# A gated linear attention and an MLP on one core: another order of work, constants as immediates, a divided last tile

## The chip, the core and the metric

The kernel runs on one core of one Trainium2 chip. A core has five engines with a queue of instructions each, worked through in order: TensorE (matrix products, the profile's PE, its weight loads PEld), VectorE (DVE), ScalarE (ACT), GpSimd (POOL) and SyncE (SP), which here only issues transfers. TensorE writes to eight PSUM banks; VectorE and ScalarE read them. The metric is the device time of one execution in microseconds, lower is better, given as the median of several runs.

## What is computed

```python
# attention, per batch (4) and head (8), 768 steps, head dim 48
mag   = sqrt(a_re**2 + a_im**2)
scale = minimum(mag, 0.999) / (mag + 1e-6)
a     = (a_re + i*a_im) * scale              # per step and channel
S     = a[t][:, None] * S + outer(k[t], v[t])   # complex state 48 x 48
y[t]  = q[t] @ real(S)
# MLP over x = the heads' y side by side (384 columns)
xn  = (x - mean(x)) / sqrt(var(x) + 1e-6) * g_ln
out = x + maximum(xn @ w_ch1, 0) @ w_ch2     # 384 -> 1536 -> 384
```

The kernel doesn't step through time. It takes the logarithm of the magnitude and the angle of every gate, sums both along time with products by triangular matrices of ones, and turns the recurrence into masked products of scaled q and k within chunks of 128 steps, with a 48 x 48 state carried from chunk to chunk.

## The kernel before, in words

The 3072 rows (4 batches of 768) are 24 chunks of 128, taken as 12 pairs, three to a batch. An operation's name tells what it does and for which pair P or chunk n; pair 0 does its gate work in two halves of four heads (are.0.0 and are.0.1), the others in one piece (are.1.0). In the order in which they depend on each other:

- **Loads (SP)**: are, aim, q, k, vf. **Gates**: ln, iv, r, r2, u, l, lc (ScalarE's logarithms and exponentials, products on VectorE or GpSimd) give the log magnitude; th is the angle (ScalarE).
- **Sums along time (TensorE)**: dec (log magnitude, products with u_e) and ph (angle; pick adds the carry car of the pair before). From their PSUM banks ScalarE makes e and en (exponentials), sin and cos (qt adds a quarter turn for the pairs 0 to 3; later pairs take the absolute value, abs). Logarithm and exponential are in one table of ScalarE, sine and arctangent in another; tab.log and tab.trig switch it.
- **Attention**: ke = k*en, qe = q*e, ks and qs (times sin and cos), v (cast). kT and qT are eight transposes each on TensorE, ksT and qsT copy them out of PSUM (some by a transposing transfer on SP instead). am are the scores, atm masks them, gm and G (with dps, decc, gs) make the state, y is the output of a chunk, x its copy.
- **MLP**: bn, rstd (normalisation), xtr and xT (transpose of x). mm1.P.g.part are the first layer's 36 products a pair (128 x 256) in three groups g, relu.P.g empties a group, mm2.n.part are a chunk's 12 products of 384 columns, ot (on VectorE; or oa on ScalarE and ot on GpSimd) scales and adds x, st stores.
- **Weights**: wl.0 loads the first layer's weights (w1b) and wl.1 the second's (w2b), both issued by GpSimd; gln is the layer norm's gain. wgc makes the matrix gc from it, wp.0 to wp.2 multiply w1b by it, and nine wc (VectorE) rewrite w1b with the gain and mean folded in. mm1 of a group waits for its three wc.
- **warm.i** are fillers: products of ones into a bank that nobody reads.

The order isn't computed by the kernel: PLAN is a table of tokens `name:engine+bank@behind`. The engines' letters are P, A, V, G and S; the number is the first PSUM bank; `@` puts a GpSimd instruction behind one of another engine. Each engine executes its tokens in the table's order, with the waits that the data, the rings of buffers (RINGS) and the banks need. Rows of the profile carry the lines of the helpers: 291 is every two-operand product of VectorE or GpSimd, 286 and 288 the copies of ScalarE and VectorE, 445 ln, 447 iv, 459 u, 463 l, 466 lc, 474 dec, 478 e and en, 482 th, 489 and 493 ph, 503 and 506 car, 511 sin, 518 qt, 522 and 534 cos, 588 kT and qT, 611 am, 672 and 675 y, 693 xtr, 726 mm1, 737 and 739 relu, 747 mm2, 761 and 759 ot, 776 the fillers, 781 the table switches, 381 wp, 385 wc, 372 gc, 361 and 363 the weights' loads, 709 and 710 rstd.

## Time and profile before

| | |
|---|---|
| median of 3 runs (lowest, highest) | 187.94 us (187.75, 189.71) |
| the profiled execution, in all | 189.19 us |
| its span, first to last instruction | 187.5 us |
| TensorE busy | 178.7 us, 95% (fillers 17.3 us of it, 128 instructions) |
| VectorE, ScalarE, GpSimd busy | 155.4, 158.3, 93.4 us |
| ScalarE's table switches | 17, 21.8 us |
| first weights' load, issue to landing | 12.0 us (second: 10.9) |
| moved by DMA | 36.08 MB, 192 GB/s in the mean |

A row of instructions in the profile reads: line, engine, operation, output<-inputs, shapes, count | busy time, mean ns of one | idle time of the engine ahead of them and what ended it. A window's row has the busy time of each engine with the number of its instructions in brackets, in the order TensorE, its weight loads, VectorE, ScalarE, GpSimd, then TensorE's granted clock, the DMA engines' share and GB/s. The chain of waits is followed back from the last instruction; its rows are start, length and what. Matmuls are pipelined: a busy time of TensorE says that one is under way, not that the array is full.

### The profile page before, as it was taken

What the parts mean: (1) busy time and instruction counts of PE and PEld (TensorE: products, weight loads), DVE (VectorE), ACT (ScalarE), POOL (GpSimd) and SP (SyncE); (2) the same over time, 40 slices, a digit from 0 to 9 for tenths busy, and PEclk for the clock granted to TensorE, in tenths of its full rate; (3) what the DMA queues carried; (4) which work ended last, traced back from release to release, by engine and by line L of the source; (5) the groups of instructions that cost most, each with busy time, mean ns of one, the idle gap of its engine ahead of it and who ended that gap; (6) DMA issues with size and microseconds to landing.
All of it is one profiled execution on the core that took longest, in us unless ns stands there. A gap on an engine that the chain in (4) does not pass through costs nothing.

```text
span 187.5 us, 5175 instructions
## 1 busy us (share of the span) xinstructions
PE 178.7 (95%) x2066; PEld 139.7 (75%) x2066; DVE 155.4 (83%) x292; ACT 158.3 (84%) x219; POOL 93.4 (50%) x117
## 2 busy tenths in 40 slices
PE   5889997999999999999999999999999999999992
PEld 3777676578866787887887887877877878787771
DVE  0379999799998999998899899999889878399431
ACT  3999999699999899999999999998999884527440
POOL 8411229756363297576572955175754174170110
PEclk9999999999999999999999999999999999999998
DMA  5999999799999998489999999996979989994223
GB/s 153 285 225 187 246 190 185 170 220 174 239 210 240 223 267 208 85 195 236 203 209 251 162 232 247 196 217 158 189 159 240 178 159 186 184 170 123 85 84 126
DMA packets 126183, 36.08 MB, mean 192 GB/s; under 512 B 121168, under 2 KB 125776, under 8 KB 126160
## 3 DMA queue, kind: packets, MB, share of 16 engines
q1 hardware_dynamic: 124208, 33.40, 84.6%
q0 software_dynamic: 1952, 2.36, 7.7%
q8 instruction: 16, 0.26, 0.6%
q14 instruction: 7, 0.06, 0.1%
HBM read 28.31 MB, written 4.72 MB: 176 GB/s over the span
## 4 chain that ended last, share of the span: by engine, by line
PE 80%; DMA 8%; ACT 7%; DVE 2%; issue 1%; DVEq 0%
PE banks L726 25%; PE banks L747 25%; DMA w1b<-in_moe_w_ch_dram 6%; PE banks L588 5%; PE banks L611 5%; PE banks L493 3%; PE banks L474 3%; PE banks L672 2%; PE banks L693 2%; PE banks L675 2%; PE banks L635 2%; DMA are<-in_a_re_dram 2%; PE banks L489 2%; ACT w L445 1%; ACT are L447 1%; ACT L781 1%
## 5 line engine op out<-in xcount | busy, mean ns | idle before, releaser
L747 PE MATMUL banks<-w2b,h 128*128 128x384 bf16 x288 | 52.5, 326 | 0.0
L726 PE MATMUL banks<-xT,w1b 128*128 128x256 bf16 x432 | 52.2, 272 | 0.0
L726 PEld LDWEIGHTS <-w1b 128*128 128x128 bf16 x432 | 41.2, 98 | 5.6
L747 PEld LDWEIGHTS <-h 128*128 128x128 bf16 x288 | 26.4, 97 | 14.9 <-ACT h L737 0.2
L737 ACT ACTIVATE h<-banks 128x1024 bf16<-128x1024 f32 x28 | 28.1, 1021 | 10.2 <-PE banks L726 9.9
L291 DVE TENSOR_TENSOR atm<-banks,mask 128x1024 bf16<-128x1024 f32 x24 | 29.2, 1218 | 4.6 <-PE banks L611 4.5
L291 POOL TENSOR_TENSOR ke<-k,en 128x384 bf16<-128x384 f32 x19 | 17.3, 915 | 17.1 <-DVE qs L291 6.9
L781 ACT ACT_TABLE_LOAD x17 | 21.8, 1283 | 1.1 <-PEq L797 0.8
L291 POOL TENSOR_TENSOR qe<-q,e 128x384 bf16<-128x384 f32 x17 | 15.4, 915 | 12.0 <-DVE qs L291 3.6
L776 PE MATMUL banks<-u_e 128*128 128x256 f16 x128 | 17.3, 290 | 2.3 <-POOL u_e L325 2.2
L776 PEld LDWEIGHTS <-u_e 128*128 128x128 f16 x128 | 12.6, 104 | 5.4 <-POOL u_e L325 1.9
L291 POOL TENSOR_TENSOR r<-aim,are 128x768 f16<-128x768 f32 x7 | 12.7, 1816 | 6.7 <-ACT are L447 5.0
L759 POOL TENSOR_TENSOR ot<-ot,x 128x384 f32<-128x384 f32 x8 | 7.3, 913 | 17.4 <-ACT ot L752 15.6
L611 PE MATMUL banks<-qsT,ksT 128*128 128x128 bf16 x192 | 14.3, 219 | 0.2 <-ACT h L737 0.2
L685 DVE BATCH_NORM_STATS2 stats<-x 128x6 f32<-128x384 bf16 x24 | 13.1, 546 | 0.0
L611 PEld LDWEIGHTS <-ksT 128*128 128x128 bf16 x192 | 12.0, 98 | 1.3 <-issue 0.5
L493 PE MATMUL banks<-th,u_th 128*128 128x384 f16 (+1 forms) x52 | 11.8, 313 | 0.9 <-ACT th L482 0.9
L761 DVE SCALAR_TENSOR_TENSOR ot<-banks,rstd,x 128x384 f32<-128x384 f32 x16 | 9.7, 610 | 3.4 <-PE banks L747 3.3
L291 POOL TENSOR_TENSOR ks<-ke,trig 128x768 bf16<-128x768 bf16 x6 | 9.8, 1640 | 5.3 <-DVE l L466 2.4
L463 DVE SCALAR_TENSOR_TENSOR l<-r,w 128x768 f16<-128x768 f16 (+1 forms) x13 | 11.5, 890 | 0.9 <-ACT r L459 0.9
L672 PE MATMUL banks<-v,atm 128*128 128x48 bf16 x192 | 12.2, 183 | 0.0
L445 ACT ACTIVATE w<-are 128x768 f32<-128x768 f32 (+1 forms) x13 | 10.1, 788 | 2.4 <-DMA are<-in_a_re_dram 2.3
(97 smaller groups left out, 376.5 us busy)
## 6 DMA issues: line engine op xcount, KB each, us to landing
k<-in_k_dram SPq DMA_DIRECT2D x24, 192.0 KB, 4.1
q<-in_q_dram SPq DMA_DIRECT2D x24, 192.0 KB, 4.2
vf<-in_v_dram SPq DMA_DIRECT2D x24, 192.0 KB, 4.2
out_dram<-ot SPq DMA_DIRECT2D x24, 192.0 KB, 3.3
are<-in_a_re_dram SPq DMA_DIRECT2D x11, 384.0 KB, 4.8
aim<-in_a_im_dram SPq DMA_DIRECT2D x11, 384.0 KB, 4.5
w1b<-in_moe_w_ch_dram POOLq DMA_DIRECT2D x1, 1152.0 KB, 12.0
w2b<-in_moe_w_ch_dram POOLq DMA_DIRECT2D x1, 1152.0 KB, 10.9
```

The costliest lines, as they stand in the source:

```text
L291: {"DVE": nc.vector, "POOL": nc.gpsimd}[eng(name)].tensor_tensor(**kw)
L445: add(f"ln.{X}", lambda S_=S_: act(out=S_("w"), in_=S_("are"), func=AF.Ln), needs=[f"are.{X}"], uses=[("are", P), ("w", P)])
L463: nc.vector.scalar_tensor_tensor(out=S_("l"), in0=S_("r2"), scalar=0.5, in1=S_("w"), op0=ALU.mult, op1=ALU.add)
L493: nc.tensor.matmul(heads(ps[:, c]), lhsT=u_th[:, c, j], rhs=step(T("th", P), j), start=False, stop=(j == R - 1), skip_group_check=True)
L611: nc.tensor.matmul(ps[:, h], lhsT=T("ksT", n)[:, h], rhs=T("qsT", n)[:, h], start=True, stop=True)
L672: nc.tensor.matmul(ps[:, h], lhsT=T("atm", n)[:, h], rhs=T("v", P)[:, c, h], start=True, stop=nfirst)
L685: nc.vector.bn_stats(out=T("stats", n), in_=T("x", n))
L726: nc.tensor.matmul(ps[:, jj], lhsT=w1b[:, dc, ts(gi * JG + jj, C)], rhs=T("xT", P)[:, dc].rearrange("p c t -> p (c t)"), start=(dc == 0), ...
L737: act(out=dst, in_=src, func=AF.Relu)
L747: nc.tensor.matmul(bank(f"o.{n}")[:, 0:DM], lhsT=T("h", P)[:, j, ts(c, C)], rhs=w2b[:, j], start=(j == 0), stop=(j == NJ - 1))
L776: g.add(f"warm.{i}", lambda i=i: nc.tensor.matmul(bank(f"warm.{i}")[:, 0:256], lhsT=u_e[:, 0, 0], rhs=u_e[:, 1].rearrange("p j t -> p (j t ...
L781: g.add(f"tab.{nm}.{i}", lambda tab=tab: nc.scalar.preload_act_table_set(tab))
```

## The change

1. PLAN is another table. 128 fillers become 29: 14 of 256 columns as before and 15 of 512 (warm.w0 to warm.w14), the first of them behind lc.1.0. Many operations change their engine: of VectorE's ReLUs there are 12, not 8; of GpSimd's qs 6, not 2; r2 goes to ScalarE six times, not twice; table switches are 15, not 17. wl.0 stands behind ke.0.0.0 (before: l.2.0), and th.1.0 ahead of the second table switch (before: behind the third).
2. The activations' constants 1, pi/2 and 1e-6 are given as numbers, no longer as 128 x 1 tiles (one_b, quarter, eps_b).
3. wgc can be done by GpSimd in one instruction, and the new table does so.
4. The last chunk's second layer is done in two column pieces, 0 to 255 (mm2.23, ot.23, st.23) and 256 to 383 (mm2.24, ot.24, st.24), in two banks with two stores.

```diff
 PLAN = """
-are.1.0:S ue:G are.0.1:S are.0.0:S pad.ks.1:G zdec:G pad.ks.0:G k.0.1:S qrow:G car0.1:G pick:G aim.0.1:S tab.log.0:A
-ln.1.0:A mask:G aim.0.0:S one:G iv.1.0:A car0.0:G aim.1.0:S cmean:G pad.ks.2:G ln.0.1:A ident:G ln.0.0:A are.2.0:S
-iv.0.1:A iv.0.0:A gln:S r.0.1:V uth:V aim.2.0:S r.0.0:V r2.0.1:V r2.0.0:V tab.trig.1:A th.0.1:A th.0.0:A k.1.0:S
...
-warm.41:P0 warm.42:P0 ph.0.1:P2 r.1.0:V ph.0.0:P0 r2.1.0:V k.0.0:S tab.log.2:A u.0.1:A pad.qs.0:G@r2.1.0 q.0.0:S
-u.0.0:A l.0.1:V u.1.0:A vf.0.0:S l.0.0:V lc.0.1:V lc.0.0:V ln.2.0:A warm.43:P1 warm.44:P1 warm.45:P1 warm.46:P1
...
-warm.57:P1 warm.58:P1 warm.59:P1 warm.60:P1 warm.61:P1 warm.62:P1 warm.63:P1 dec.0.1:P5 l.1.0:V q.0.1:S dec.0.0:P4
-en.0.1:A5 lc.1.0:V e.0.1:A5 q.1.0:S car.0.1:V2 iv.2.0:A warm.64:P1 warm.65:P1 warm.66:P1 warm.67:P1 warm.68:P1
-dec.1.0:P6 pad.qs.1:G@lc.1.0 car.0.0:V0 q.1.1:S e.0.0:A4 r.2.0:V e.1.0:A6 vf.0.1:S en.0.0:A4 r2.2.0:V warm.69:P1
-warm.70:P1 warm.71:P1 warm.72:P1 warm.73:P1 warm.74:P1 warm.75:P1 warm.76:P1 warm.77:P1 warm.78:P1 dps.1:P5 dps.0:P1
-en.1.0:A6 ke.0.0.0:V are.3.0:S decc.1:V5 u.2.0:A qe.0.1.0:V k.1.1:S ke.0.1.0:V qe.1.0.0:V aim.3.0:S qe.0.0.0:V l.2.0:V
-tab.trig.3:A th.1.0:A q.2.1:S wl.0:G@l.2.0 lc.2.0:V sin.0.1:A2 warm.79:P3 warm.80:P3 warm.81:P3 warm.82:P3 warm.83:P3
...
-warm.103:P3 warm.104:P3 warm.105:P3 warm.106:P3 warm.107:P3 warm.108:P3 warm.109:P3 ph.1.0:P6 wgc:V sin.0.0:A0
-th.2.0:A decc.0:V1 k.2.0:S qs.0.1.1:V dec.2.0:P4 ke.1.0.0:V car.1.0:A6 qt.0.1:P2 ks.0.0.1:V sin.1.0:A6 qt.0.0:P0
-qe.1.0.1:V qs.0.0.1:V cos.0.0:A0 warm.110:P1 warm.111:P1 qt.1.0:P6 v.0:V cos.0.1:A2 ks.0.1.1:V cos.1.0:A6 ks.0.0.0:V
-qs.0.0.0:V qs.0.1.0:V ks.0.1.0:V warm.112:P0 warm.113:P0 warm.114:P0 warm.115:P0 warm.116:P0 warm.117:P0 warm.118:P0
-warm.119:P0 warm.120:P0 warm.121:P0 qT.0:P6 qs.1.0.1:V kT.1:P1 qs.1.0.0:V qT.1:P7 qsT.0:V6 tab.log.4:A ln.3.0:A
-ke.1.0.1:G@qs.1.0.0 kT.0:P0 qsT.1:V7 qT.2:P6 en.2.0:A4 ks.1.0.1:G@qs.1.0.0 qT.3:P2 ksT.1:V1 e.2.0:A4 gm.0:P7 ksT.0:V0
-iv.3.0:A warm.122:P3 warm.123:P3 warm.124:P3 am.1:P4 qsT.3:V2 ks.1.0.0:G am.0:P0 G.0:A7 atm.1:V4 ph.2.0:P2 vf.1.1:S
-atm.0:V0 gm.1:P7 y.1:P4 tab.trig.5:A sin.2.0:A2 k.2.1:S r.3.0:G G.1:V7 warm.125:P5 warm.126:P5 warm.127:P5 wp.2:P5
-qsT.2:A6 x.1:V4 y.0:P0 vf.1.0:S qt.2.0:P2 wc.2.2:V5 x.0:A0 wp.1:P7 cos.2.0:A2 wc.2.0:V5 aim.4.0:S qe.2.0.1:G xtr.1:P0
-kT.2:P1 wc.1.0:V7 xT.1:A0 xtr.0:P6 r2.3.0:G are.4.0:S th.3.0:A wp.0:P2 wc.2.1:V5 kT.3:P3 ksT.2:A1 q.2.0:S wc.1.2:V7
-ph.3.0:P4 wc.1.1:V7 ke.2.0.0:G xT.0:A6 vf.2.0:S ksT.3:A3 am.2:P0 wc.0.2:V2 v.1:G mm1.0.1.1:P6 atm.2:V0 sin.3.0:A4
...
-mm1.11.0.0:P0 ot.19:G ot.20:V2 st.18:S mm1.11.0.1:P0 bn.23:V st.20:S mm1.11.1.0:P4 st.19:S relu.11.0:A0 mm1.11.1.1:P4
-mm1.11.2.1:P6 relu.11.1:V4 mm1.11.2.0:P6 mm2.22.0:P0 relu.11.2:A6 mm2.22.1:P0 rstd.11:A mm2.22.2:P0 oa.21:A3
-mm2.23.0:P2 ot.22:V0 ot.21:G mm2.23.1:P2 st.22:S mm2.23.2:P2 st.21:S ot.23:V2 st.23:S
+ue:G are.1.0:S are.0.0:S are.0.1:S pick:G aim.1.0:S pad.qs.1:G qrow:G car0.1:G pad.ks.0:G aim.0.0:S tab.log.0:A
+ln.1.0:A pad.ks.2:G aim.0.1:S mask:G iv.1.0:A ident:G k.1.0:S ln.0.0:A cmean:G ln.0.1:A zdec:G car0.0:G pad.qs.0:G
+iv.0.1:A vf.0.0:S iv.0.0:A k.0.1:S r.1.0:V are.2.0:S r.0.0:V tab.trig.1:A th.1.0:A r.0.1:V gln:S uth:V th.0.0:A
+r2.0.1:V r2.0.0:V th.0.1:A ph.0.0:P1 aim.2.0:S r2.1.0:G@r2.0.0 ph.0.1:P0 q.0.1:S car.0.1:V0 car.0.0:V1 tab.log.2:A
+u.0.0:A u.0.1:A l.0.0:V q.0.0:S u.1.0:A lc.0.0:V l.0.1:V dec.0.0:P2 vf.0.1:S lc.0.1:V en.0.0:A2 l.1.0:V k.0.0:S
+ln.2.0:A lc.1.0:V iv.2.0:A q.1.1:S warm.w0:P3 warm.0:P3 warm.1:P3 dec.1.0:P4 pad.ks.1:G@lc.1.0 e.0.0:A2 r.2.0:V
+ph.1.0:P6 q.1.0:S en.1.0:A4 e.1.0:A4 dec.0.1:P2 r2.2.0:V k.1.1:S qe.0.0.0:V e.0.1:A2 car.1.0:V6 are.3.0:S en.0.1:A2
+warm.w1:P3 warm.2:P3 warm.3:P3 dps.0:P4 v.0:V u.2.0:A qe.0.1.0:V aim.3.0:S decc.0:V4 ke.0.1.0:V q.2.0:S ke.0.0.0:V
+wl.0:G@ke.0.0.0 l.2.0:V tab.trig.3:A sin.0.1:A0 q.2.1:S sin.0.0:A1 warm.w2:P3 warm.w3:P3 warm.4:P3@u.2.0 warm.w4:P3
+warm.w5:P3 warm.w6:P3 warm.w7:P3 warm.w8:P3 warm.5:P3 warm.6:P3 warm.7:P3 qt.0.1:P0 sin.1.0:A6 dps.1:P4 lc.2.0:V
+qt.0.0:P1 ks.0.0.1:V dec.2.0:P2 qs.0.1.1:V cos.0.0:A1 qe.1.0.0:V cos.0.1:A0 qt.1.0:P6 qs.0.0.1:V th.2.0:A qs.0.0.0:V
+qs.0.1.0:V ks.0.1.1:V cos.1.0:A6 warm.w9:P0 warm.8:P0 warm.9:P0 qT.1:P0 ks.0.0.0:V ks.0.1.0:V qT.0:P1 qsT.1:V0
+decc.1:A4 ke.1.0.0:G@ks.0.1.0 kT.1:P5 qsT.0:V1 kT.0:P6 gm.0:P0 qe.1.0.1:V tab.log.4:A e.2.0:A2 qs.1.0.0:V ksT.1:V5
+G.0:A0 ke.1.0.1:G@qs.1.0.0 en.2.0:A2 ksT.0:V6 warm.w10:P1 warm.w11:P1 warm.w12:P1 warm.w13:P1 warm.w14:P1 warm.10:P1
+warm.11:P1 warm.12:P1 gm.1:P0 am.1:P4 ks.1.0.0:V ln.3.0:A ph.2.0:P2 ks.1.0.1:V iv.3.0:A atm.1:V4 qs.1.0.1:G@ks.1.0.1
+kT.3:P6 kT.2:P7 G.1:V0 y.1:P4 ksT.2:V7 am.0:P0 wgc:G tab.trig.5:A sin.2.0:A2 qT.2:P5 k.2.0:S atm.0:V0 x.1:A4
+warm.13:P7 qt.2.0:P2 xtr.1:P4 qsT.2:V5 cos.2.0:A2 wp.1:P7 vf.1.1:S r.3.0:G xT.1:V4 y.0:P0 ksT.3:A6 wc.1.2:V7 am.2:P2
+vf.1.0:S qT.3:P1 wc.1.1:V7 x.0:A0 wp.0:P4 pad.qs.2:G k.2.1:S wc.1.0:V7 th.3.0:A xtr.0:P0 wp.2:P5 r2.3.0:G atm.2:V2
+qsT.3:A1 are.4.0:S ph.3.0:P6 xT.0:A0 wc.2.1:V5 aim.4.0:S am.3:P2 qe.2.0.1:G car.3.0:A6 mm1.0.1.0:P0 wc.2.0:V5
+sin.3.0:A6 are.5.0:S mm1.0.1.1:P0 atm.3:V2 wl.1:G@mm1.0.1.0 v.1:A qt.3.0:P6 vf.2.0:S relu.0.1:A0 ke.2.0.0:G wc.2.2:V5
...
+mm1.11.1.1:P0 oa.20:A3 st.21:S mm1.11.0.0:P4 ot.20:G mm1.11.0.1:P4 ot.19:G st.20:S mm1.11.1.0:P0 relu.11.0:A4
+mm1.11.2.1:P2 st.19:S relu.11.1:V0 mm1.11.2.0:P2 mm2.22.0:P4 relu.11.2:A2 mm2.22.1:P4 rstd.11:A mm2.22.2:P4
+mm2.23.0:P5 ot.22:V4 mm2.23.1:P5 st.22:S mm2.23.2:P5 mm2.24.0:P0 ot.23:V5 mm2.24.1:P0 mm2.24.2:P0 st.23:S ot.24:V0
+st.24:S
@@ -235,6 +226,7 @@
     ND = DM // C
     HALF = C // R
     JG = 4
+    CUT = 256
     NG = NJ // JG
     INV2PI = 1.0 / (2.0 * PI)
 
@@ -302,10 +294,7 @@
     u_e = pool.tile([C, R, R, C], FP16, name="u_e")
     pick = pool.tile([C, C], FP16, name="pick")
     mask = pool.tile([C, C], BF16, name="mask")
-    one_b = pool.tile([C, 1], FP32, name="one_b")
-    quarter = pool.tile([C, 1], FP32, name="quarter")
     half_n = pool.tile([C, R], FP32, name="half_n")
-    eps_b = pool.tile([C, 1], FP32, name="eps_b")
     qrow = pool.tile([C, DM], FP16, name="qrow")
     cmean = pool.tile([C, C], FP32, name="cmean")
     gc = pool.tile([C, ND, C], BF16, name="gc")
@@ -314,10 +303,7 @@
     w2b = pool.tile([C, NJ, DM], BF16, name="w2b")
 
     def c_one():
-        nc.gpsimd.memset(one_b, 1.0)
-        nc.gpsimd.memset(quarter, PI / 2)
         nc.gpsimd.memset(half_n, -0.5)
-        nc.gpsimd.memset(eps_b, 1e-6)
 
     def c_ue():
         nc.gpsimd.memset(u_e, 1.0)
@@ -365,6 +351,10 @@
     g.add("gln", lambda: nc.sync.dma_start(out=gln, in_=moe_g_ln.rearrange("(dc p) -> p dc", p=C)))
 
     def wgc():
+        if eng("wgc") == "POOL":
+            nc.gpsimd.tensor_tensor(out=gc, in0=cmean.unsqueeze(1).to_broadcast([C, ND, C]),
+                                    in1=gln.unsqueeze(2).to_broadcast([C, ND, C]), op=ALU.mult)
+            return
         for dc in range(ND):
             if eng("wgc") == "ACT":
                 nc.scalar.mul(out=gc[:, dc], in_=cmean, mul=gln[:, ds(dc, 1)])
@@ -456,8 +446,8 @@
                 else:
                     tt(f"r2.{X}", out=S_("r2"), in0=S_("r"), in1=S_("r"), op=ALU.mult)
             add(f"r2.{X}", f_r2, needs=[f"r.{X}"], uses=[("r", P), ("r2", P)])
-            add(f"u.{X}", lambda S_=S_: act(out=S_("r2"), in_=S_("r2"), func=AF.Ln, bias=one_b),
-                needs=[f"r2.{X}", "one"], uses=[("r2", P)])
+            add(f"u.{X}", lambda S_=S_: act(out=S_("r2"), in_=S_("r2"), func=AF.Ln, bias=1.0),
+                needs=[f"r2.{X}"], uses=[("r2", P)])
 
             def f_l(S_=S_):
                 nc.vector.scalar_tensor_tensor(out=S_("l"), in0=S_("r2"), scalar=0.5, in1=S_("w"),
@@ -533,8 +523,8 @@
                 add(f"abs.{X}", f_abs, needs=[f"ph.{X}"], uses=[("sh", P)], ps=(f"ph.{X}", nb))
                 add(f"cos.{X}", lambda fs=fs: act(
                     out=T("trig", P)[:, 0, :, fs], in_=T("sh", P)[:, :, fs], func=AF.Sin,
-                    scale=-TWO_PI_SAFE / TURN, bias=quarter),
-                    needs=[f"abs.{X}", "one"], uses=[("sh", P), ("trig", P)])
+                    scale=-TWO_PI_SAFE / TURN, bias=PI / 2),
+                    needs=[f"abs.{X}"], uses=[("sh", P), ("trig", P)])
 
 
             for nm, src, dc_ in (("ke", "k", "en"), ("qe", "q", "e")):
@@ -706,7 +696,7 @@
         def f_rstd():
             t = T("rstd", P)
             if eng(f"rstd.{P}") == "ACT":
-                act(out=t, in_=T("mv", P)[:, :, 1], func=AF.Ln, bias=eps_b)
+                act(out=t, in_=T("mv", P)[:, :, 1], func=AF.Ln, bias=1e-6)
                 act(out=t, in_=t, func=AF.Exp, scale=-0.5)
                 return
             nc.gpsimd.tensor_scalar(out=t, in0=T("mv", P)[:, :, 1], scalar1=1e-6, scalar2=None,
@@ -741,41 +731,48 @@
                 needs=[f"mm1.{P}.{gi}.0", f"mm1.{P}.{gi}.1"], uses=[("h", P)], ps=(o, 2))
         for c in range(R):
             n = P * R + c
-            for part in range(NG):
-                def f_mm2(n, c, part):
-                    for j in range(part * JG, part * JG + JG):
-                        nc.tensor.matmul(bank(f"o.{n}")[:, 0:DM], lhsT=T("h", P)[:, j, ts(c, C)],
-                                         rhs=w2b[:, j], start=(j == 0), stop=(j == NJ - 1))
-                add(f"mm2.{n}.{part}", lambda n=n, c=c, part=part: f_mm2(n, c, part),
-                    needs=[f"relu.{P}.{part}", "wl.1"] + ([f"mm2.{n}.{part - 1}"] if part else []),
-                    uses=[("h", P)], ps=(f"o.{n}", 1))
-            add(f"oa.{n}", lambda n=n, c=c: nc.scalar.mul(
-                out=T("ot", n), in_=bank(f"o.{n}")[:, 0:DM], mul=T("rstd", P)[:, ds(c, 1)]),
-                needs=[f"mm2.{n}.{NG - 1}", f"rstd.{P}"], uses=[("rstd", P), ("ot", n)],
-                ps=(f"o.{n}", 1))
-
-            def f_ot(n, c):
-                if eng(f"ot.{n}") == "POOL":
-                    nc.gpsimd.tensor_tensor(out=T("ot", n), in0=T("ot", n), in1=T("x", n), op=ALU.add)
-                else:
-                    nc.vector.scalar_tensor_tensor(
-                        out=T("ot", n), in0=bank(f"o.{n}")[:, 0:DM], scalar=T("rstd", P)[:, ds(c, 1)],
-                        in1=T("x", n), op0=ALU.mult, op1=ALU.add)
-            add(f"ot.{n}", lambda n=n, c=c: f_ot(n, c),
-                needs=[f"oa.{n}", f"mm2.{n}.{NG - 1}", f"rstd.{P}", f"x.{n}"],
-                uses=[("rstd", P), ("x", n), ("ot", n)], ps=(f"o.{n}", 1))
-            add(f"st.{n}", lambda n=n, c=c: nc.sync.dma_start(
-                out=out[b].rearrange("(c p) e -> p c e", p=C)[:, pp * R + c], in_=T("ot", n)),
-                needs=[f"ot.{n}"], uses=[("ot", n)])
+            tail = P == NP - 1 and c == R - 1
+            for N, ws in (((n, slice(0, CUT)), (n + 1, slice(CUT, DM))) if tail else ((n, slice(0, DM)),)):
+                for part in range(NG):
+                    def f_mm2(n, N, ws, c, part):
+                        for j in range(part * JG, part * JG + JG):
+                            nc.tensor.matmul(bank(f"o.{N}")[:, ws], lhsT=T("h", P)[:, j, ts(c, C)],
+                                             rhs=w2b[:, j, ws], start=(j == 0), stop=(j == NJ - 1))
+                    add(f"mm2.{N}.{part}", lambda n=n, N=N, ws=ws, c=c, part=part: f_mm2(n, N, ws, c, part),
+                        needs=[f"relu.{P}.{part}", "wl.1"] + ([f"mm2.{N}.{part - 1}"] if part else []),
+                        uses=[("h", P)], ps=(f"o.{N}", 1))
+                add(f"oa.{N}", lambda n=n, N=N, ws=ws, c=c: nc.scalar.mul(
+                    out=T("ot", n)[:, ws], in_=bank(f"o.{N}")[:, ws], mul=T("rstd", P)[:, ds(c, 1)]),
+                    needs=[f"mm2.{N}.{NG - 1}", f"rstd.{P}"], uses=[("rstd", P), ("ot", n)],
+                    ps=(f"o.{N}", 1))
+
+                def f_ot(n, N, ws, c):
+                    o, xs = T("ot", n)[:, ws], T("x", n)[:, ws]
+                    if eng(f"ot.{N}") == "POOL":
+                        nc.gpsimd.tensor_tensor(out=o, in0=o, in1=xs, op=ALU.add)
+                    else:
+                        nc.vector.scalar_tensor_tensor(
+                            out=o, in0=bank(f"o.{N}")[:, ws], scalar=T("rstd", P)[:, ds(c, 1)],
+                            in1=xs, op0=ALU.mult, op1=ALU.add)
+                add(f"ot.{N}", lambda n=n, N=N, ws=ws, c=c: f_ot(n, N, ws, c),
+                    needs=[f"oa.{N}", f"mm2.{N}.{NG - 1}", f"rstd.{P}", f"x.{n}"],
+                    uses=[("rstd", P), ("x", n), ("ot", n)], ps=(f"o.{N}", 1))
+                add(f"st.{N}", lambda n=n, ws=ws, c=c: nc.sync.dma_start(
+                    out=out[b].rearrange("(c p) e -> p c e", p=C)[:, pp * R + c, ws], in_=T("ot", n)[:, ws]),
+                    needs=[f"ot.{N}"], uses=[("ot", n)])
 
     for P in range(NP):
         pair_ops(P)
 
 
-    for i in range(128):
+    for i in range(14):
         g.add(f"warm.{i}", lambda i=i: nc.tensor.matmul(
             bank(f"warm.{i}")[:, 0:256], lhsT=u_e[:, 0, 0], rhs=u_e[:, 1].rearrange(
                 "p j t -> p (j t)"), start=True, stop=True), needs=["ue"], ps=(f"warm.{i}", 1))
+    for i in range(15):
+        g.add(f"warm.w{i}", lambda i=i: nc.tensor.matmul(
+            bank(f"warm.w{i}"), lhsT=u_e[:, 0, 0], rhs=u_e.rearrange("p c j t -> p (c j t)"),
+            start=True, stop=True), needs=["ue"], ps=(f"warm.w{i}", 1))
     for i in range(40):
         for nm, tab in (("log", "natural_log_exp_and_others"), ("trig", "trig_and_small")):
             g.add(f"tab.{nm}.{i}", lambda tab=tab: nc.scalar.preload_act_table_set(tab))
```

## The prediction

> **What bounds the kernel now.** I read the chain of waits first. By engine it is 80% TensorE, 8% DMA, 7% ScalarE. In order of time it has two halves, and its longest pieces show where they meet:

> ```profile
> 10.03 1.10 ACT L781
> 11.32 1.95 ACT r L459 x3
> ...
> 19.87 0.88 DVE l L463
> 20.75 0.30 issue
> 21.05 11.98 DMA w1b<-in_moe_w_ch_dram
> 33.08 0.81 PE banks L381 x3
> ...
> 40.13 1.03 ACT h L737
> 41.20 0.61 PE banks L611 x8
> ...
> 180.05 3.91 PE banks L747 x24
> 183.99 0.62 DVE ot L761
> ```

> Until 21.05 us a chain of small ScalarE and VectorE steps decides when GpSimd issues the load of the first weights (wl.0). The load lands 11.98 us later. From 33.08 to 183.99 us every long piece but one is a TensorE row. The windows by stage (TensorE's busy time is the second number) say the same:

> ```profile
> 30.00:35.00 5.00, 3.61 (x48) 2.18 (x47) 3.84 (x6) 3.44 (x5) 4.41 (x4) 1.00 0.75 148
> 60.00:80.00 20.00, 20.00 (x231) 15.86 (x230) 19.72 (x37) 19.08 (x26) 13.40 (x14) 1.00 0.84 199
> 100.00:120.00 20.00, 20.00 (x257) 15.68 (x256) 18.54 (x35) 19.05 (x31) 10.34 (x9) 1.00 1.10 216
> ```

> So after 45 us nothing is left to win: TensorE is full. It can only be lost there, since VectorE and ScalarE stand at 18 to 20 of 20 us. The time is: start of the weight products (33.1), plus the TensorE work still to do then, plus its holes, plus the tail from 183.99 to 187.5. I count TensorE work by the chain's paces: 3.96/36 = 0.110 us a first-layer matmul, 3.91/24 = 0.163 a second-layer one, 0.45 a group of eight transposes or score matmuls. Counted so, 149.1 us are left at 33.08 in the old order; 150.9 passed, so 1.8 us are holes, of which 0.9 lie between 33 and 43.3 (TensorE waits for a ReLU to free banks at 40.6 to 41.2).

> **The parts that leave the path alone.** The 99 fillers that go (128 rows, 17.3 us busy) stood in front of waits and, at 31.2 us, in front of the weights' landing: removing their time gives nothing by itself. The immediates shorten 26 ScalarE instructions:

> ```profile
> L445 ACT ACTIVATE w<-are 128x768 f32<-128x768 f32 x11 | 9.2, 839 | 2.4 <-DMA are<-in_a_re_dram 2.3
> L459 ACT ACTIVATE r<-r,one_b 128x768 f16<-128x768 f16 x11 | 10.3, 938 | 0.5 <-DVE r L291 0.4
> ```

> Two logarithms of one size differ by 0.10 us, and only one reads a constant's tile. 13 of L459, 8 of L534 and 5 of L709 give 2.6 us; two table loads fewer (17 to 15) give another 2 x 1.28. ScalarE has these 5 us free later, where it is not what TensorE waits for; only four logarithms (0.4 us) lie ahead of wl.0. If the float is kept in a tile all the same, that is 0; nothing makes it a loss. New work on GpSimd (the gc product, a 128x384 row: 0.92 us) stands behind qs.1.0.1 and is done near 32.2, ahead of the weights. If that cover goes, the first product waits for it.

> **The tail.** The last output tile's 12 matmuls of 384 columns become 12 of 256 and 12 of 128, the same columns: 1.95 us either way. The last VectorE instruction then has 128 columns, not 384. Its 0.62 us becomes at least 0.28 (the 128x128 row of L372) and at most 0.62: I take 0.3 saved. The other piece's store is issued while the last piece is computed (an issue takes 0.33 to 1.03 us there), so it may cost the last store up to 0.3.

> **The front, step by step.** Back to back, an instruction starts about 0.08 us before the end of the one ahead of it (two 0.55 us rows take 1.02), and I use that pace. The new order makes pair 1's arctangent (0.84) before the second table switch, so the logarithms of pair 0 begin at 12.0, not 11.32, and u.1.0 ends at 13.65. Its aim tile is behind the same bytes as the tile that had come by 7.38 before, so r.1.0 at 7.4 and th.1.0 at 9.07 fit.

> TensorE is slower here. The fillers' own rows show it (first number in brackets: matmuls in the stretch; the granted clock, after the busy times, is 1.00 in both):

> ```profile
> 2.20:4.20 2.00, 1.98 (x10) 1.39 (x10) 1.00 1.05 272
> 5.80:7.00 1.20, 1.20 (x13) 1.08 (x12) 1.00 1.03 270
> ```

> Sixteen started from 2.2 to 5.4 us, one in 0.21, each 418 ns long; from 5.8 us on it is one in 0.11, 272 ns long. The pace doubled 3.6 us after the first matmul. With no filler ahead, ph.0's twelve 192-column matmuls run from 10.2 at half pace, 0.16 each (0.21 x 192/256), to 12.3 with the last one's drain. On VectorE car.0.1 and car.0.0 wait for them in front of l.0.0, so l.0.0 starts at 12.9 (0.4 late), dec.0.0 at 13.7 and, halved, ends at 14.5; ScalarE idles until then. Then en.0.0, ln.2.0 and iv.2.0 (to 16.6), e.0.0 (17.0); dec.1.0 from 15.7 to 17.2; en.1.0 and e.1.0 to 18.75. ph.1.0 and dec.0.1 follow on TensorE: 18.5 if the pace has doubled by 17, 19.7 if not. e.0.1, en.0.1 and u.2.0 are done at 20.25 or 21.35. VectorE needs 3.1 us from qe.0.0.0 (18.1) to the end of ke.0.0.0: 21.2, or 22.05. So wl.0, though now ahead of l.2.0, is issued at **21.4 to 22.3**, against 21.05, and lands by the same 11.98 at 33.4 to 34.3. w2b took 10.9; 11.98 has the same neighbours, so I keep it. SyncE's queue gets k.1.0 and vf.0.0 ahead of are.2.0 and aim.2.0; at its 0.7 to 1.0 us an issue and 4.2 to landing are.2.0 is there by 12.5 (needed at 14.9), and q.0.0, now its 14th issue, by 17.4 (needed at 18.1), the tightest.

> VectorE, now busy without a hole, reaches xT.1 at about 33.5, and x.1 on ScalarE is done at 32.7: both just ahead of the weights. By then TensorE has done 0.95 us more of its work than before (two groups of kT, qt.2 and xtr.1 done, one of qT not yet). From the first product (33.4) I find the first-layer matmuls at 38.05 (38.41 before), short waits for wc.2.2 and wc.0.1 (0.1 and 0.25) and 9.1 us of work done by 43.05, with the 0.95 ahead 10.1, against 9.1 before: **1.0 us gained** if the pace doubles at 17, nothing if at 20. Half of it is my value: -0.5. Later TensorE has one group of eight transposes more (qT.16, 0.45) and three fewer (xtr.20, 0.17): +0.3. Tail -0.3. For in-order waits in the later stages I take +0.2: between a producer and its consumer the new order leaves as much TensorE work as the old one (the tightest places, y to xtr and am to y, have 0.07 us above the VectorE row between them, against -0.03 in the old). The bounds are 0 and, as the old order's holes after 43.3 sum to 0.9, about 3 (three times that).

> Sum: -0.5 + 0.3 - 0.3 + 0.2 = -0.3 us. The profiled execution had a span of 187.5 and 189.19 us in all, 1.7 around the span; the median of the three other runs is 187.94. On the profiled time it is 188.9, on the median **187.6 us**: no change that can be measured. About 1% is what a measurement tells here (the three runs reach from 187.75 to 189.71).

> **Rivals.**
> - *Slower: TensorE's clock.* The fillers hold the pace. If few of them let it fall back between 25 and 33 us, where TensorE will work in bursts between VectorE's copies, then it costs: late doubling 1.0, the groups that VectorE waits for there (qT.1, kT.3 and kT.2, qT.2: four times 0.45) 1.8, and 3.6 us of half pace from the first product, 1.8. Of this some 1.0 hides beneath the load: 3.6 us, 191.2. It decides from the point where a stretch between two groups is long enough to lose the pace. Against it: between 8.7 and 11.0 us TensorE stood for much of the time and its 192-column matmuls still took 244 ns. [...] Chance 0.12.
> - *Slower: new waits in the full stages.* VectorE gets 12 ReLUs instead of 8 (1.22 us each) and GpSimd 12 products of 1.64 us instead of 8; one instruction late stands before all behind it. 1 to 3 us: 188.6 to 190.8. For it: 18 to 20 busy of 20. Against: the load moves by about 1 us on VectorE in all and falls by 6 on ScalarE. Chance 0.18.
> - *Faster: the front falls into place.* The pace doubles already at ph.0 (dec.0.0 and dec.1.0 full: 0.55), the full 1.0 of the front is gained, and the weights come in w2b's 10.9 us, of whose 1.1 VectorE, due only at 33.5, leaves 0.5; the tail and the extra transposes cancel and no new wait comes: 187.94 - 1.0 - 0.55 - 0.5 = 185.9, 185.3 with the rest of the 1.1. Chance 0.17.
> - *The change doesn't do what it says* (constants kept in tiles): +0.4, inside the forecast.

> **How the numbers follow.** Forecast 0.53, alone 186.5 to 188.6. Faster by over 1% (under 186.1): the faster rival, 0.17. Slower by over 1% (over 189.8): the clock 0.12 and half of the new waits, 0.22. The rest 0.61. The range from 185.6 to 190.5 leaves out the clock's 0.12 and some 0.05 of the faster case.

> **What would show it.** ph.0's 192-column matmuls near 0.37 (0.244 x 418/272) rather than 0.244 us. wl.0's issue at 21.4 to 22.3, its landing 12 us later, the first L381 row right behind. TensorE 20 of 20 from 45 us on. The logarithm with the immediate 0.84. I am wrong if wl.0 is issued before 20.5 or after 23, if TensorE waits over 1 us in a later stage, or if the transposes between 25 and 33 run at 0.9 a group.

## The result, and the profile after

| | before | after |
|---|---|---|
| median, same chip, 20 runs each | 188.69 us (187.56 to 192.68) | 189.81 us (189.21 to 191.04) |
| ratio after to before, 95% interval | | 1.0067 [1.0046, 1.0087] |
| profiled execution in all, span | 189.19, 187.5 us | 189.64, 187.9 us |
| last matmul's end, from there to the end of the span (the tail) | 183.95, 3.53 us | 185.05, 2.88 us |
| TensorE, VectorE, ScalarE, GpSimd busy | 178.7, 155.4, 158.3, 93.4 us | 171.7, 158.1, 152.3, 98.8 us |
| first weights' load: issue, length | 21.05, 11.98 us | 22.37, 10.7 us |
| second weights' load: issue, length | 39.91, 10.9 us | 39.73, 13.51 us |
| first weight product, first first-layer matmul | 33.08, 38.41 us | 33.94, 38.59 us |

The change makes the kernel 0.67% slower: less than the 1% at which I said that a change can be told from none, but its interval lies clear of 1. 18 of the old order's 20 runs spread from 187.56 to 189.71; 19 of the new one's 20 lie between 189.2 and 190.0. The expectations further down give the tails as 3.69 and 2.93: they count from the end of the matmul before the last.

The chain of waits of the kernel after, in order of time (start, length, what):

```profile
7.80 1.28 ACT L778
...
21.03 1.03 DVE ke L283 x2
22.05 0.88 DVE l L453
25.35 1.80 PE banks L578 x32
...
39.73 13.51 DMA w2b<-in_moe_w_ch_dram
53.28 4.06 PE banks L739 x24
...
113.96 1.11 issue
123.14 1.13 DVE h L729
125.06 1.22 DVE atm L283
127.11 0.95 DVE qs L283 x2
...
181.12 3.94 PE banks L739 x36
...
185.09 0.35 DVE ot L754
```

The first weights' load is no longer in it: it landed at 33.1, ahead of the first product at 33.94, and TensorE's own queue decides there. In its place stands the second weights' load, for which TensorE waits at 53 us, and between 114 and 128 us a stretch in which VectorE, with a ReLU (h) in it, takes a large part. The windows by stage (TensorE's busy time second; after the five busy times its granted clock):

```profile
30.00:35.00 5.00, 4.92 (x73) 3.50 (x72) 4.90 (x9) 4.44 (x7) 4.26 (x4) 1.00 0.95 188
60.00:80.00 20.00, 20.00 (x237) 15.45 (x235) 17.96 (x36) 19.67 (x27) 13.39 (x16) 1.00 0.86 200
100.00:120.00 20.00, 20.00 (x243) 15.29 (x242) 19.27 (x37) 19.13 (x27) 13.01 (x12) 1.00 1.00 213
```

TensorE shows 20 of 20 again. That it started 243 matmuls from 100 to 120 us and not 257 is another mix of work, not a loss. But a busy time that counts each 256-column matmul as 272 ns, where one starts every 0.11 us, hides short waits. So I counted holes: the time between the ends of two neighbouring matmuls, less the pace of the second (0.11 us for 256 columns). From 100 to 120 us they are 0.38 us before and 0.35 after; elsewhere they differ, and that gives the account below. The second column is against the shown profile of before; the third against another execution of the same kernel, profiled in the runs below, which at 188.42 us lies nearer its median.

| term, us | predicted | after less shown before (189.19) | after less before again (188.42) |
|---|---|---|---|
| front (what is left of TensorE's later end) | -0.5 | -0.44 | +0.5 |
| eight transposes more, three fewer (by their count and pace) | +0.3 | +0.28 | +0.28 |
| holes from 33 us on, without the wait for the first weights (2.30 and 2.47 before, 3.56 after) | +0.2 | +1.26 | +1.09 |
| tail | -0.3 | -0.65 | -0.65 |
| sum | -0.3 | +0.45 | +1.2 |

The groups of the immediates' rows (busy, mean ns of one):

```profile
L435 ACT ACTIVATE w<-are 128x768 f32<-128x768 f32 x11 | 9.3, 842 | 2.2 <-DMA are<-in_a_re_dram 2.2
L449 ACT ACTIVATE r<-r 128x768 f16<-128x768 f16 x11 | 9.2, 839 | 0.1
```

The logarithm that took 938 ns with a constant's tile takes 839 without one.

### The profile page after: what moved, and what is told of

It is laid out like the page before. It is cut to its first block, busy times and chain, and to the rows that moved or that the text cites. A ratio compares the mean times of both kernels' runs of the same rounds, so it can differ in the third digit from the quotient of the medians.

```text
span 187.9 us, 5017 instructions
## 1 busy us (share of the span) xinstructions
PE 171.7 (91%) x1983; PEld 131.4 (70%) x1984; DVE 158.1 (84%) x287; ACT 152.3 (81%) x219; POOL 98.8 (53%) x117
## 4 chain that ended last, share of the span: by engine, by line
PE 72%; DMA 9%; DVE 8%; ACT 6%; issue 2%; DVEq 0%
PE banks L739 22%; PE banks L716 19%; DMA w2b<-in_moe_w_ch_dram 7%; PE banks L578 6%; PE banks L601 5%; PE banks L483 4%; PE banks L464 3%; PE banks L662 2%; PE banks L479 2%; DMA are<-in_a_re_dram 2%; PE banks L683 2%; PE banks L625 2%; PE banks L665 2%; ACT are L437 1%; ACT w L435 1%
## 5 line engine op out<-in xcount | busy, mean ns | idle before, releaser
L739 PE MATMUL banks<-w2b,h 128*128 128x384 bf16 (+2 forms) x300 | 52.7, 319 | 0.3 <-DMA w2b<-in_moe_w_ch_dram 0.3
L727 ACT ACTIVATE h<-banks 128x1024 bf16<-128x1024 f32 x24 | 24.4, 1023 | 11.0 <-PE banks L716 11.0
L283 POOL TENSOR_TENSOR r<-aim,are 128x768 f16<-128x768 f32 x8 | 14.6, 1819 | 12.8 <-ACT are L437 9.7
L729 DVE TENSOR_SCALAR h<-banks 128x1024 bf16<-128x1024 f32 x12 | 14.6, 1216 | 4.0 <-PE banks L716 4.0
L283 POOL TENSOR_TENSOR qe<-q,e 128x384 bf16<-128x384 f32 x14 | 12.7, 919 | 7.1 <-ACT x L278 3.6
L483 PE MATMUL banks<-th,u_th 128*128 128x384 f16 (+1 forms) x52 | 12.9, 337 | 3.0 <-ACT th L472 3.0
L479 PE MATMUL banks<-car,pick 128*128 128x384 f16 (+2 forms) x26 | 8.8, 338 | 7.1 <-POOL car L338 7.1
L601 PEld LDWEIGHTS <-ksT 128*128 128x128 bf16 x192 | 11.9, 98 | 1.7 <-DVE atm L283 0.2
L464 PE MATMUL banks<-l,u_e 128*128 128x384 f16 (+1 forms) x52 | 10.9, 336 | 2.1 <-DVE l L456 2.1
L483 PEld LDWEIGHTS <-u_th 128*128 128x128 f16 x52 | 5.5, 106 | 9.8 <-DVE u_th L316 6.5
L283 POOL TENSOR_TENSOR qs<-qe,trig 128x768 bf16<-128x768 bf16 x6 | 9.8, 1641 | 4.2 <-DVE qs L283 2.2
L435 ACT ACTIVATE w<-are 128x768 f32<-128x768 f32 (+1 forms) x13 | 10.2, 791 | 2.2 <-DMA are<-in_a_re_dram 2.2
## 6 DMA issues: line engine op xcount, KB each, us to landing
w1b<-in_moe_w_ch_dram POOLq DMA_DIRECT2D x1, 1152.0 KB, 10.7
```

The source lines that it names most:

```text
L283: {"DVE": nc.vector, "POOL": nc.gpsimd}[eng(name)].tensor_tensor(**kw)
L464: nc.tensor.matmul(heads(ps[:, c]), lhsT=u_e[:, c, j], rhs=step(T("l", P), j), start=(j == 0), stop=(j == R - 1))
L479: nc.tensor.matmul(ps[:, c], lhsT=pick[rows], rhs=T("car", P)[rows, fs], start=(c == 0 or NS == 1), stop=False, skip_group_check=True)
L483: nc.tensor.matmul(heads(ps[:, c]), lhsT=u_th[:, c, j], rhs=step(T("th", P), j), start=False, stop=(j == R - 1), skip_group_check=True)
L601: nc.tensor.matmul(ps[:, h], lhsT=T("ksT", n)[:, h], rhs=T("qsT", n)[:, h], start=True, stop=True)
L727: act(out=dst, in_=src, func=AF.Relu)
```

## The experiments

All ratios are to the kernel before, measured on the same chip in the same series; between series the median of the kernel before moved from 188.51 to 188.83, so a difference of some tenths of a microsecond between variants of two series is rough. The edits show the tokens that change, with the rest of their lines left out; the lines of code that make more or fewer fillers aren't shown.

**The kernel before, again.** No edit.

> The kernel before, unchanged, profiled once more. Its times lie at 187.6 to 187.9 or at 188.7 to 189.7 us; the profile shown was taken at 189.19. Theory 'the weights' landing decides': in the old order TensorE stood 1.55 us (31.7 to 33.1) for the first weights, so an execution near 187.8 shows a load of 10.5 to 11 us instead of 11.98 and a first weight product near 31.8; one near 189.2 shows the same 12. Rival 'it is elsewhere': the first weight product stays at 33.1 and the difference lies after 45 us or around the span.

188.42 us; the median of before in this series was 188.64 (23 runs, 187.56 to 191.29). The first weights' load was issued at 20.9 and took 11.2 us, not 11.98, TensorE waited 0.75 us for it, not 1.55 (counted as holes; 0.59 and 1.39 idle), and the first first-layer matmul came at 37.45, 0.96 earlier. The execution that I predicted from was one with a late load.

**The old order with its first load earlier.**

```diff
-tab.trig.3:A th.1.0:A q.2.1:S wl.0:G@l.2.0 lc.2.0:V
+tab.trig.3:A th.1.0:A q.2.1:S lc.2.0:V
-en.1.0:A6 ke.0.0.0:V are.3.0:S
+en.1.0:A6 ke.0.0.0:V wl.0:G@ke.0.0.0 are.3.0:S
```

> The old order with one thing changed: the first weights' load stands behind ke.0.0.0 (17.5 us) instead of l.2.0 (20.75). Theory 'the weights' landing decides': the load is issued 3.2 us earlier and lands at 29 to 30.5, so the first product starts when its predecessors on TensorE end (31.7): the times fall together at 187.6 to 187.9, ratio 0.992 to 0.997 to the mixed times of before. Rival 'it is elsewhere': no change of the spread, ratio 0.999 to 1.001; rival 'the early load takes the transfers' turns': q, k and vf come late, slower by 0.3 to 1%.

188.98 us, 1.0027 [0.9990, 1.0064]. The load was issued 3.4 us earlier, at 17.62, took 10.2, and won nothing. In the profiled execution (190.92 us in all) the chain of waits runs through transfers and not through the weights:

```profile
13.20 4.81 DMA q<-in_q_dram
18.06 0.04 issue
18.11 0.56 DVE qe L291
...
30.14 0.80 ACT e L478
```

The last row stands late because of another transfer, the load of an are tile that was issued at 18.1, behind the early weights' load, and took 10.6 us. ScalarE's logarithm of that tile (w, L445) waited for it in the same execution (in all, times, longest wait in us):

```profile
ACT w L445 <- DMA are<-in_a_re_dram: 2.4, 1, 2.4
```

Pair 2's exponentials (e, en) stand behind this logarithm in ScalarE's order: they began at 29.45 (26.96 in the profile of before), and the first product came at 33.8, without a wait for the weights, which had landed at 27.8. So in this execution the landing of the weights was no free lever: other transfers came late. That the early load took their turns fits it, but it is argued from one execution, among the slowest of its twelve.

**The old order without its first 64 fillers.**

```diff
-warm.0:P0 warm.1:P0 warm.2:P0
...
-warm.62:P1 warm.63:P1
```

> The old order without its first 64 fillers (those ahead of ph.0 and of dec.0). Theory 'half pace in the front': the matmuls run at half pace until 16 to 20 us, dec.0 and dec.1.0 take 0.6 and 0.6 us more, ph.1.0 isn't on the path there; wl.0 is issued 0.7 to 1.2 us later (21.8 to 22.3), time 0.6 to 1.2 us more: 189.2 to 189.9, ratio 1.003 to 1.007. Rival 'fillers are only filler': ratio 0.999 to 1.001.

189.14 us, 1.0015 [0.9981, 1.0049]. TensorE ran at half pace until 16.6 (five 256-column fillers took 1.07 us from 14.6) and the third table switch came at 19.58, 1.1 late; but the load, issued at 22.15, took only 9.9, and the first product came at 32.6, right behind the matmuls ahead of it. The theory's 189.2 to 189.9 isn't shown, but its lower half lies inside the interval. In this execution the late clock used up the time that TensorE otherwise stood waiting for the load.

**The new code with the old order.** Immediates and divided last tile, old table.

```diff
-mm2.23.2:P2 st.21:S ot.23:V2 st.23:S
+mm2.23.2:P2 st.21:S mm2.24.0:P4 ot.23:V2 mm2.24.1:P4 mm2.24.2:P4 st.23:S ot.24:V4 st.24:S
```

> The old order with the new code: constants as immediates, the last chunk's second layer in two pieces, all 128 fillers. Theory: the tail from the last matmul to the end is 2.95 us instead of 3.69 (0.7 less), and the four logarithms ahead of wl.0 bring it 0.3 forward: 0.7 to 1.0 us less, ratio 0.9945 to 0.9965. Rival 'the tail's gain in the new kernel came from its order': ratio 0.998 to 1.000.

188.46 us, 0.9972 [0.9938, 1.0006]; tail 3.32 us, 0.2 less than before. Its holes are those of the old order (1.44 us after 45 us). The loss lies in the new table, not in the code.

**The new order with 59 fillers ahead.**

```diff
+warm.14:P3 warm.15:P3
...
+warm.55:P3 warm.56:P3
 ph.0.0:P1 aim.2.0:S r2.1.0:G@r2.0.0 ph.0.1:P0
+warm.57:P3 warm.58:P3
...
+warm.71:P3 warm.72:P3
 q.0.1:S
```

> The new order with 59 fillers of 256 columns put back, 43 ahead of ph.0.0 and 16 between ph.0.1 and dec.0.0. Theory 'half pace in the front': ph.0 ends at 11.6 instead of 12.4, dec.0.0 takes 0.6 instead of 0.8, dec.1.0 0.8 instead of 1.44, the third table switch comes 1.0 to 1.3 us earlier (20.82 to 19.7), the first weight product at 33.0 instead of 33.9, the time 0.7 to 1.0 us less: 188.8 to 189.1, ratio to the new order's 0.995. Rival 'the loss is in the later waits': the front moves the same way, but the time by less than 0.3 us, since the second weights' landing (53.2) or a VectorE queue takes it back.

189.34 us, 1.0029 [0.9993, 1.0065], with two groups of runs near 188.55 and 189.35. The third table switch came at 19.37, 1.45 us earlier than in the new kernel. The lead was lost again in the profiled execution. Its windows:

```profile
20.00:23.80 3.80, 3.06 (x25) 1.50 (x23) 3.73 (x9) 3.72 (x7) 1.00 (x1) 1.00 1.02 260
23.90:27.20 3.30, 3.30 (x28) 2.89 (x28) 2.60 (x8) 3.10 (x5) 0.90 (x1) 0.50 1.10 192
27.40:30.00 2.60, 2.60 (x42) 1.97 (x40) 2.50 (x5) 1.89 (x3) 0.92 (x1) 1.00 1.11 212
```

The granted clock falls to 0.50 from 23.8 to 27.2, and the first two groups of transposes take 1.91 us, not the 1.05 of the new kernel. Ahead of the fall TensorE had short holes (0.64 us the longest) and matmuls of one column or one row. The fall isn't all of it: of the four runs near 189.35 two have a mean granted clock of 0.991, the profiled one among them, and two 0.999 or more.

**The same with 6 fillers of 512 columns in the middle.**

```diff
 dps.1:P4
+warm.w15:P3
 lc.2.0:V qt.0.0:P1 ks.0.0.1:V
+warm.w16:P3 warm.w17:P3 warm.w18:P3
 dec.2.0:P2
+warm.w19:P5
...
 cos.1.0:A6
+warm.w20:P0
 warm.w9:P0
```

> The new order with the 59 early fillers and six more of 512 columns between 21.5 and 25 us (around qt.0, dec.2.0, qt.1.0 and ahead of qT.1). Theory 'half pace in the front': in the run with early fillers alone TensorE's matmuls fell back to half pace from 23.9 to 27.2 us, and its lead of 0.9 to 1.4 us was gone at 27; held at full pace, qsT.1 starts near 25.0, x.1 near 31.7, the first weight product at 32.7 to 33.0, and all times lie at 188.4 to 188.6, the lower group of that run. Rival 'ScalarE's and VectorE's list is too long, not TensorE too slow': the first product stays at 33.8 or later and the time at 189.3. Rival 'fillers get in the way': over 189.5.

189.10 us, 1.0012 [0.9982, 1.0042]: 0.7 us back, its interval just apart from the new kernel's (1.0042 against 1.0046). The clock stayed at 1.00; the first product came at 33.60 and the first first-layer matmul at 38.25. That is between the theory (32.7 to 33.0, 188.4 to 188.6) and the first rival (33.8, 189.3): the clock gives back a part, and ScalarE's and VectorE's lists are not ruled out for the rest.

**The new order with the second load ungated.**

```diff
-wl.1:G@mm1.0.1.0
+wl.1:G
```

> The new order with the second weights' load no longer behind mm1.0.1.0: GpSimd issues it at 37.7 instead of 39.73. Theory 'the second weights hold mm2': they land at 51.2 instead of 53.24, TensorE's standing of 0.65 us at 52.6 to 53.3 goes, time 0.4 to 0.7 us less (189.1 to 189.4). Rival 'another wait is next' (state, scores or ReLU are due at the same time): under 0.2 us. Rival 'the transfers only change turns': the load lands at 53 all the same, 0 us.

189.77 us, 1.0080 [1.0055, 1.0104], six runs. The load was issued at 38.36, and the 0.33 us in which the new kernel's second layer waits for it,

```profile
53.28 1.46 PE L739 MATMUL banks<-w2b,h 128*128 128x384 bf16 x8 [0.33 <-DMA w2b<-in_moe_w_ch_dram]
```

are gone; holes from 45 to 60 us fall from 0.89 to 0.37. The median doesn't move. In the profiled execution the half pace lasted to 20.5 (a 512-column filler took 0.43 us at 20.0, in the new kernel 0.21 from 21.0 on) and the front was 0.73 later, which ate the gain; whether that holds for the other runs isn't shown.

**Both, and the quarter turn earlier.** The 65 added fillers, the ungated load, and pair 1's qt ahead of dec.2.0.

```diff
-wl.1:G@mm1.0.1.0
+wl.1:G
-qt.0.0:P1 ks.0.0.1:V
+qt.0.0:P1 qt.1.0:P6 ks.0.0.1:V
-cos.0.1:A0 qt.1.0:P6 qs.0.0.1:V
+cos.0.1:A0 qs.0.0.1:V
```

> The new kernel with the 59 fillers ahead and 6 in the middle of the earlier run (189.10), and two waits taken out: the second weights' load no longer stands behind the first first-layer matmul on GpSimd, and the quarter turn of pair 1 stands ahead of dec.2.0 in TensorE's order. If the new order's loss is the late front plus the holes behind 33 us (the theory), the hole in front of the second layer at 52.6 to 53.2 (0.32 there) and ScalarE's waits of 0.2 and 0.45 at 22.4 and 24.0 go: TensorE ends 0.3 to 0.6 earlier, 188.5 to 188.8, no slower than before. If holes that close are only handed on to the next place (the rival, as the run with the ungated load alone suggested with 189.77 against 189.81), it stays at 189.0 to 189.2.

188.73 us, 0.9992 [0.9963, 1.0021]; ten of the twelve runs lie between 188.59 and 188.84. The new order's loss is gone: 1.1 us, and its interval lies apart from the new kernel's. The fillers had given 0.7 of it; that the two moves give the other 0.4 isn't shown, since the interval of the run with the 65 fillers alone overlaps with this one. The two other runs were at 189.93 and 190.34, and the latter is the profiled one. It shows a reason:

```profile
10.50:11.80 1.30, 1.29 (x15) 1.26 (x15) 0.10 (x1) 1.28 (x2) 0.74 (x1) 1.00 1.13 261
12.00:15.00 3.00, 3.00 (x18) 2.29 (x16) 2.53 (x7) 1.84 (x4) 0.00 (x0) 0.50 1.14 251
```

TensorE had stood from 8.55 to 10.51, and at 11.9 its clock halved for 3.4 us, although it was at work again. The run at 189.93 has the same mean granted clock, 0.991; the ten others have 0.998 or more.

**17 more fillers over that stand.**

```diff
 warm.56:P3
+warm.73:P3 warm.74:P3
...
+warm.88:P3 warm.89:P3
 ph.0.0:P1
```

> The last version of the new order (59 + 6 fillers, second weights' load ungated, quarter turn earlier: ten runs at 188.59 to 188.84, two at 189.9 and 190.3) with 17 more fillers ahead of pair 0's angle sums, so that TensorE, which stood from 8.4 to 10.5 us there and fell to half pace at 11.9 in the profiled execution, works through to 10.3. If that stand cost the two late runs their pace (the theory), no run is above 189.2 but for disturbed ones, the pace is full from 5.5 us on, and the median is 188.6 to 188.7. If the fall has another cause, some runs stay at 189.9 to 190.3. If the added fillers push ph.0 back, all runs are 0.2 to 0.5 later.

189.37 us, 1.0034 [1.0000, 1.0067]: no faster, and three runs above 190. The clock didn't fall, not in these three either (0.999 or more in the mean), but it rose only at 7.3 in the profiled execution, one of the three (5.1 in the profile before), so that the row of fillers ran past the work it was to lead to:

```profile
2.22 9.19 PE L769 MATMUL banks<-u_e 128*128 128x256 f16 x60 [2.22 <-POOL u_e L311]
```

Pair 0's angle sums started at 11.24, 0.7 later than in the profile of the version without them. At the 0.11 us a filler of full pace these 60 would take 6.6 us, at the 0.21 of half pace 12.6 (an estimate from the paces in the profile of the kernel before); they took 9.19. A fixed number of fillers is a stretch of time only if the clock is known.

**The new order without any filler.**

```diff
-warm.w0:P3 warm.0:P3 warm.1:P3
...
-warm.13:P7
```

> The new order without any of its 29 fillers. Theory 'half pace in the front': half pace lasts into the transposes at 25 us or longer, each group of eight takes 0.9 instead of 0.45, the first weight product comes at 35 to 36, and 1 to 2 us more in all: 190.8 to 192. Rival 'the 29 do nothing': 189.8 as the new order.

192.55 us, 1.0177 [1.0116, 1.0238], four runs. Half pace from 7.1 to 18.8, and again from 22.2 to 29.0 (granted clock 0.50), where the transposes stand (16 in 1.89 us, 1.05 in the new kernel); first first-layer matmul at 40.2, 1.6 us later than in the new kernel. Another 1.9 us are holes behind 160 us: at 169.2 and 180.2 first-layer matmuls wait for transposing transfers of x (idle 0.45 and 1.10 us). Why these came late isn't shown, so that of the 2.7 us by which the median rose only the front's part can be put down to the fillers.

**The last tile undivided.** The new kernel with the last chunk as the others are:

```diff
-            tail = P == NP - 1 and c == R - 1
+            tail = False
...
-mm2.23.2:P5 mm2.24.0:P0 ot.23:V5 mm2.24.1:P0 mm2.24.2:P0 st.23:S ot.24:V0 st.24:S
+mm2.23.2:P5 ot.23:V5 st.23:S
```

> The new kernel with the last chunk's second layer in one piece of 384 columns and one store, as before; all else stays. From the last matmul's end to the end of the span: 2.93 us divided. If the divided tile alone makes the tail shorter, it is 3.7 again, as in the old order, and the time 190.5. If half of it came from the order of the last stores (in the old order the divided tile gave 3.38, 0.3 less), the tail is 3.3 to 3.4 and the time 190.2. If the dividing gives nothing, 189.8.

190.42 us, 1.0099 [1.0065, 1.0133], which overlaps with the new kernel's interval; tail 3.60 us, against 2.88 divided. In the profiled execution the second load took 14.53 us from 39.97 and TensorE waited 1.52 us for it, so part of its span is that; the runs spread from 189.8 to 191.6. By the tail alone dividing is worth 0.72 us.

**The old order, one store out of the last queue.** On top of the new code with the old order:

```diff
 relu.11.1:V4
+ot.21:V3 st.21:S
 mm1.11.2.0:P6 mm2.22.0:P0 relu.11.2:A6 mm2.22.1:P0 rstd.11:A mm2.22.2:P0
-oa.21:A3
-mm2.23.0:P2 ot.22:V0 ot.21:G mm2.23.1:P2 st.22:S mm2.23.2:P2 st.21:S
+mm2.23.0:P2 ot.22:V0 mm2.23.1:P2 st.22:S mm2.23.2:P2
```

> The old order with the immediates and the divided last tile (earlier run: 188.46, tail 3.38), and chunk 21's result taken by one VectorE instruction ahead of the last ReLUs instead of ScalarE and GpSimd, its store issued before the last layer's matmuls, so that SyncE's queue holds three stores at the end and not four. If the last store waited in that queue (the theory), the tail falls to 2.9 to 3.0 and the time to 188.0, 0.3% below before. If the store's own landing sets it, 3.4 stays and 188.4 to 188.6.

188.91 us, 1.0009 [0.9972, 1.0046]; the tail stays at 3.33. The theory of the waiting store falls. In this order the span ends 2.94 us after the last VectorE instruction, in the new kernel 2.49. The last store isn't the difference: it landed 1.54 us after its issue here and 1.55 there. The 0.4 us lie behind the landing (1.36 us to the end of the span here, 0.91 there), and what makes them stays open. No version is shown to beat the kernel before.

## Why the prediction was wrong

The range held the time and the likeliest case, no difference of 1%, came; the sign of the small difference was wrong. **Two steps failed.** Against the very execution that the sum started from, the front and the transposes came as worked out and the tail gave more, and the in-order waits alone, taken at +0.2 and measured at +1.26, turn -0.3 into +0.45. Against a more usual execution of the kernel before the front failed too: +0.5 in place of -0.5. That the time still came near is in part luck, since the tail gave 0.35 us more than forecast.

- **The base.** I subtracted from one execution (189.19) and put the difference on the median of three (187.94). Of 20 runs the median is 188.69. That is 0.75 of the 2.2 us between 187.6 and 189.81, and no fault of the change. The same execution had a load of 11.98 us; in four others of the old order it took 9.9 to 11.9 with the issue at 20.9 to 22.2.
- **The front's steps** came nearly as worked out: ph.0 at half pace (0.36 us a 192-column matmul, predicted 0.37), the clock doubled at 18.1 (between 17 and 20, an estimate of mine), wl.0 issued at 22.37 (21.4 to 22.3), first product at 33.94 (33.4), first first-layer matmul at 38.59 (38.05). **What failed there** is "1.0 us gained if the pace doubles at 17, nothing if at 20": it was reckoned against an old front with a late load. On that execution the new front gains 0.44; on the more usual one it loses 0.5, and with the clock held from the start (59 and 6 fillers) 0.34 us comes back at the first first-layer matmul. I took 11.98 us as the load's length and not as a draw.
- **"Landing by the same 11.98".** It took 10.7. In all the profiles, loads issued after 22 us took 9.9 to 10.8 us, those issued between 20.9 and 21.5 took 9.5 to 12.0; and neither the issue moved 3.4 us ahead nor the one moved 1.1 back moved the time.
- **In-order waits, +0.2: the other step that failed.** They were +1.1 to +1.26, inside the bounds of 0 and 3. The reason given, that "between a producer and its consumer the new order leaves as much TensorE work as the old one", was read off from y to xtr and from am to y; the waits came elsewhere. Of the 0.89 us of holes from 45 to 60 us (0.19 or 0.35 before) 0.49 stand ahead of the first second-layer matmul. I never priced that step: the diff put wl.1 behind mm1.0.1.0, its issue stayed at 39.7, and I had only the 10.9 us of the shown execution, where the other profiles with an issue near 39 to 40.6 us have 11.9 to 14.5. From 120 to 140 us (0.03 before, 0.47 after) two groups of transposes wait, for VectorE's qs (0.23) and for GpSimd's ks (0.21), which itself waited for VectorE's ke; qs and ke stand behind a ReLU and an atm on VectorE:

```profile
PEld L578 <- DVE qs L283: 0.4, 1, 0.4
POOL ks L283 <- DVE ke L283: 1.8, 1, 1.8
```

  With the second load's wait, this is the rival of new waits, at the low end of its 1 to 3 us. What each of these waits is worth in time isn't shown: ungating the load alone took its wait away and left the median where it was.
- **"After 45 us TensorE is full"** was read off busy times of 20 of 20, which hid the holes in both kernels: 1.44 us before, 2.58 after.
- **Tail, -0.3.** It was -0.65. The VectorE row gave 0.27 of it (0.62 to 0.35 us), as counted. I feared a loss of up to 0.3 by the extra store; instead the last store, smaller now, landed 0.3 us sooner after its issue (KB, us from issue to landing; before, the median of the last three stores, and after):

```profile
out_dram<-ot SPq DMA_DIRECT2D x3, 192.0 KB, 1.9
out_dram<-ot SPq DMA_DIRECT2D x1, 64.0 KB, 1.6
```

  In the five profiles with an undivided last tile the last store landed 1.85 to 1.94 us after its issue, in the nine with a divided one 1.54 to 1.64. In the old order the same edit gave both parts but only 0.2 in all: there the span ended 1.35 us after that landing, not 0.99 as before it, and why isn't shown.
- **Extra transposes** (+0.28) and **immediates** (0.10 us each, off the path) were right. gc was done at 33.2 and not 32.2, still ahead of the first product.
- **The rival of the clock** didn't occur in the new kernel's profile (transposes at 25.20 in 1.05 us for 16). It did in three variants, between 22 and 29 us in two of them, one with 59 fillers more and one with none. Its condition, one stretch between two groups that is long enough, wasn't what decided: with 59 fillers more the clock fell behind holes of 0.64 us at most. The last section has what the traces show. In the chances, 0.12 and half of 0.18 make 0.21, not 0.22.

## What to carry to other kernels

Before taking a difference from one profile, ask whether that execution is a usual one: where the path goes through a transfer, as here through the first weights' load (9.9 to 12.0 us in five profiles with the old order and its issue at 20.9 to 22.2), its length is a draw and needs the profiles of two executions or more. A full engine in a busy-time view can still lose a microsecond (2.58 us of holes after 45 us here); measure the gaps between the ends of its matmuls. Where fillers are thinned out, the question is not their time but the clock they hold up (0.50 from 22.2 to 29.0 us in the run without any), so count the work that is left to TensorE there; and a moved load deserves a line of its own in the sum even if its issue stays where it was.
